# Sums of the second weights: made by adding DMAs into SBUF in the second expert phase, instead of in DRAM in the first

## The chip, the cores and the metric

One core of a Trainium2 chip. The metric is the time of one execution on the device in microseconds (us). The kernel before takes 2145.75 us, the median of 3 runs (2145.28 to 2146.46).

## The reference

`x` has 2048 rows (tokens) of 512. The kernel computes a gated mix of a Fourier transform of `x` and a mixture of eight experts in which all eight are used (K = 8 of E = 8):

```
g = sigmoid((x * gate_w).sum(-1))
a = dft_seq_re @ (x @ dft_hid_re.T) - dft_seq_im @ (x @ dft_hid_im.T)
w = softmax(x @ w_gate)                       # one weight for each of 8 experts
b = sum_e w[:, e] * (silu(x @ w1[e]) @ w2[e])  # w1: 8 x 512 x 1376, w2: 8 x 1376 x 512
out = g * a + (1 - g) * b
```

All values are float32. The matmuls run on pairs of a high and a low part: a "high" copy made by ScalarE (a Copy into float32r), a "low" remainder made by a subtraction, and three matmuls for each product (high × high, high × low, low × high). So every matmul operand costs one ScalarE instruction and one subtraction on VectorE or GpSimd.

## The kernel before

The 8 × 1376 rows of the expert weights form 86 chunks of 128 hidden units. The program runs in four stages. First the transform along the sequence (0 to 322 us of the profile), then the projections with `wd` (322 to 418 us). Then comes the **first expert phase** (418 to 1317 us): 29 rounds (`plan_round`), each of 20 fast-multiplication products (chains A to F, `SEQ`) on up to three chunks, which gives the hidden values. Each round loads its block of `w1` and makes sums and splits of it (GpSimd lines 1064 and 1079, ScalarE line 1077, loads in lines 1033, 1035 and 1070). Lines 1152 and 1178 combine the products, line 1230 copies PSUM banks that are needed again, 1168 applies the silu, and the values and their combinations are stored to DRAM in `hd` (lines 1184, 1206 and 1221).

The **second expert phase** (1317 to 2140 us) multiplies the hidden values by `w2` with a 2 × 2 Strassen–Winograd scheme. Chunks come in 43 pairs (`NPAIR`), and a matrix of weights is split into four quarters 11, 12, 21, 22, of which one block in DRAM (`w2d`) holds 128 × 512 values, enough for two pairs; there are 22 blocks (`NB2`). The seven products need these weights (`FORMS`, line 1351): product 1 takes 11, 4 takes 22, 2 takes 12, and the others take sums of quarters: s1 = 21 + 22 (product 5), s2 = s1 + 11 (product 6), s3 = 11 + 21 (product 7) and s4 = s2 + 12 (product 3). The products are computed in groups that share loads of hidden values: `GROUPS = ((1, 7), (6, 4), (3, 5), (2,))`. Within a group the loop runs over the 43 pairs; the second product of a pair follows `SKEW` = 2 pairs behind the first. One product of one pair is 12 matmuls of 128 × 512 in four PSUM banks, so a pair of a two-product group is 24 matmuls and a block of weights lasts for 48. The 12 or 24 matmuls need hidden values from DRAM (`plan_pair_h`, loads of 512 KB in line 1437, one or two for each pair; a subtraction of two of them in line 1451 for products 7, 4 and 5; splits in lines 1458 and 1462) and a block of weights (`plan_pair_w`, loads of 256 KB in line 1415, split in lines 1420 and 1425). When a group ends, its banks go to eight accumulators of 512 KB in SBUF (`accb`; the transform's part, loaded from `yd` and multiplied by the gate in line 1366): straight by VectorE, or by a ScalarE copy (line 1489) and additions on GpSimd (both line 1377). The last accumulations are stored to the output (line 1384).

**The sums before.** `plan_sums` (lines 1317 to 1345) makes s1 to s4 in DRAM (`sd`) during the first expert phase, four blocks at a time: SP copies a quarter (line 1325, 1 MB), GpSimd's queue adds another to it by an adding DMA (line 1328, `accum_op=add`), SP copies that sum as the start of the next, and so on. For each group of blocks there are four copies and four adding DMAs; two of the four copies, c2 and c4, read what an adding DMA wrote.

**What sets the order.** `Plan` (line 98) is a list scheduler that runs when the program is built: each operation has an engine, a duration, a due time, a release time `rel`, its dependencies, and buffers of a ring ("RW" for blocks of the second phase). For each engine it takes the ready operation with the earliest due time, and gives it a buffer. A DMA is taken to end `size / GBPS` after the DMAs before it, plus 2.2 us (line 277). The resulting order is written out; `pin` keeps it for ScalarE, VectorE, GpSimd (its DMAs too) and the first matmul of each triple. Loads and copies on SP aren't pinned, and can be put earlier by the layer that records the program. At run time each engine, and SP's queue, executes in order: an instruction whose wait isn't over holds everything behind it on that engine.

Of the kernel before, what the change touches and what calls it, by code (L numbers as in the profile page):

```python
# [97 lines left out]
class Plan:  # L98
# [49 lines left out]
    def run(self, t0):  # L148
# [59 lines left out]
        while left:  # L208
# [19 lines left out]
            while again:  # L228
                again = False
                for e in engines:  # L230
# [56 lines left out]
def fnet_moe_kernel(ctx: ExitStack, tc: tile.TileContext, x, xT, cT, wd, w1d, w2d, wg, out):  # L287
# [27 lines left out]
    sd = dram.tile([4, NB2, P, 2, 256], F32, name="sd")  # L315
# [11 lines left out]
    def pin(ins):  # L327
        tc.keep_in_program_order(ins)
# [986 lines left out]
    sdone = {}  # L1315

    def plan_sums(q, t):
        lo, hi = 4 * q, min(4 * q + 4, NB2)
        size = 2 * MB / 2 * (hi - lo)

        def flat(a):
            return a.rearrange("b (p r) q c -> (b p) (r q c)", r=4)

        def copy(dst, src, due, deps):
            return load(due, lambda: nc.sync.dma_start(flat(dst), flat(src)), size, deps=deps, rel=due)

        def plus(dst, src, due, deps):
            return op("POOL", 1.2, due, lambda: pin(nc.gpsimd.dma_start(flat(dst), flat(src), accum_op=add,
                                                                        max_dma_last_dim=4096)),
                      deps, rel=due, size=size)  # L1330

        S = [sd[s_, lo:hi] for s_ in range(4)]
        W11, W12, W21, W22 = (w2d[s_, lo:hi] for s_ in range(4))
# [8 lines left out]
        sdone[q] = {1: a1, 2: a2, 3: a3, 4: a4}  # L1342

    for q in range((NB2 + 3) // 4):
        plan_sums(q, T1 + 30 + 104 * q)
# [43 lines left out]
    SKEW, NEARLY = 2, 2  # L1389
    units = []  # L1390
    for gi, ms in enumerate(GROUPS):
        for p in range(NPAIR):
            units.append((gi, 0, p))
            before = (gi, p - SKEW) if p >= SKEW else (gi - 1, NPAIR + p - SKEW)
            if before[0] >= 0 and len(GROUPS[before[0]]) == 2:
                units.append((before[0], 1, before[1]))
    need_at = {u: T2 + 4 * UNIT * n for n, u in enumerate(units)}

# [4 lines left out]
    def plan_pair_w(gi, p):  # L1403
        ms, need = GROUPS[gi], need_at[gi, 0, p]
        src_, lob, hib = X("RW"), X(), X()
        lo_ = []
        for j, m in enumerate(ms):
            key = FORMS[m][1]
            dep = []
            if key[0] == "s":  # L1410
                s_ = int(key[1])
                dep, src = [sdone[p // 8][s_]], sd[s_ - 1, p // 2]
            else:
                src = w2d[("11", "12", "21", "22").index(key), p // 2]
            lo_.append(load(need - 10, lambda j=j, src=src: nc.sync.dma_start(f(src_)[:, j, :],
                                                                            src.rearrange("p q c -> p (q c)")),
                            MB, deps=dep, bufs=[src_], rel=need - 24))
# [3 lines left out]
                lo_, [src_, hib])  # L1421
        early = gi == 0 and p < 4
# [7 lines left out]
    def plan_pair_h(gi, p):  # L1430
# [10 lines left out]
        for m in ms:  # L1441
# [6 lines left out]
            early = gi == 0 and p < 3  # L1448
# [130 lines left out]
```

## Time and profile before

| | before |
|---|---|
| time, median of 3 runs | 2145.75 us |
| time of the profiled execution | 2146.88 us |
| its span (first to last instruction) | 2144.9 us |
| PE busy | 2046.7 us (95%), 8848 matmuls |
| DVE busy | 1643.6 us (77%) |
| ACT busy | 1046.0 us (49%) |
| POOL busy | 845.4 us (39%) |
| mean granted TensorE clock | 0.982 |
| DMA, mean | 233 GB/s, 500.47 MB |

PE is the TensorE's matmuls, PEld its weight loads, DVE is VectorE, ACT ScalarE, POOL GpSimd, SP the engine that issues most DMAs; PEq, SPq and POOLq are the queues of PE, SP and POOL. A row of the timeline is: start, duration, engine, line, operation, output<-inputs, shape, and in brackets the idle time before it with what ended it. Names are those of the buffers: `psp` are PSUM banks, `tc`, `tg` and `tw` temporary buffers, `wfs` split first weights, `hd`, `sd` and `w_dram` tensors in DRAM (`w_dram` stands for `w1` and `w2`), names that begin with `xf` the big SBUF buffers. The granted clock is the share of its full clock that TensorE was given. Matmuls are pipelined, so a stage is best judged by the time it takes for a count of matmuls.

### The profile page before, as it was taken

Reading aid. Unit: us, or ns where it says so; the run is one execution under the profiler, and the core shown is the slowest. Engines: PE = TensorE matmul, PEld = TensorE weight load, DVE = VectorE, ACT = ScalarE, POOL = GpSimd, SP = SyncE. Lnnn points to the kernel's source line nnn. Section 1 sums busy time; section 2 is a strip of 40 time slices with the busy share of each in tenths; the row PEclk is TensorE's granted clock in tenths of the full one; section 3 lists DMA queues with packets and bytes.
Section 4 is the critical chain, followed back from the end, with each engine's and each line's share of the span. In section 5 each row is a group of like instructions: output and inputs, shape, how many; then the busy total and the mean of one; then the engine's idle time right before and its main releaser. Section 6 shows DMA issues by size and latency. Waiting matters only on the chain.

```text
span 2144.9 us, 26751 instructions
## 1 busy us (share of the span) xinstructions
PE 2046.7 (95%) x8848; PEld 1672.3 (78%) x8848; DVE 1643.6 (77%) x1870; ACT 1046.0 (49%) x1463; POOL 845.4 (39%) x785
## 2 busy tenths in 40 slices
PE   9999999999988898989899998999999999999999
PEld 7887888777766676767778887888888888888887
DVE  8999994876856666677778877998798779877663
ACT  6545543544544444444455555544544444444442
POOL 0010100487776776777788985131140004000110
PEclk9999999999999999999999999999999999999999
DMA  9887766557676766757786559987768777877681
GB/s 359 306 311 261 243 234 220 192 171 209 190 226 184 210 184 184 224 161 222 201 247 181 195 187 331 354 278 252 229 225 274 243 237 240 292 240 241 206 323 68
DMA packets 200546, 500.47 MB, mean 233 GB/s; under 512 B 22196, under 2 KB 37044, under 8 KB 200024
## 3 DMA queue, kind: packets, MB, share of 16 engines
q1 hardware_dynamic: 194248, 475.45, 66.0%
q0 software_dynamic: 6016, 23.07, 6.5%
q8 instruction: 69, 1.13, 0.2%
q14 instruction: 69, 0.57, 0.1%
q10 hardware_dynamic: 144, 0.26, 0.1%
HBM read 391.66 MB, written 153.17 MB: 254 GB/s over the span
## 4 chain that ended last, share of the span: by engine, by line
PE 48%; DMA 2%; DVE 1%; POOL 1%; issue 0%; ACT 0%; SPq 0%; DVEq 0%; POOLq 0%; ACTq 0%
PE psp L340 16%; PE psp L344 16%; PE psp L343 16%; DMA tc<-gTd 0%; DMA hd<-tg 0%; DMA hd<-tc 0%; DMA hd<-tw 0%; DVE tc L1178 0%; POOL tg L1064 0%; POOL wfs2n L1079 0%; DVE psp L1152 0%; POOL wfs0n L1079 0%; ACT tg L1230 0%; POOL wfs1nnnn L1079 0%; DVE tc L1201 0%
## 5 line engine op out<-in xcount | busy, mean ns | idle before, releaser
L1168 ACT ACTIVATE psp<-psp 128x512 f32<-128x512 f32 x287 | 164.7, 582 | 247.5 <-DVE psp L1152 188.9
L1377 POOL TENSOR_TENSOR xfx6n<-xfx6n,tc 128x512 f32<-128x512 f32 x2 | 4.0, 1985 | 416.8 <-ACT tc L1489 416.8
L1230 ACT ACTIVATE tc<-psp 128x512 f32<-128x512 f32 x90 | 53.3, 596 | 62.4 <-PE psp L344 44.4
L1152 DVE TENSOR_TENSOR psp<-psp,tc 128x512 f32<-128x512 f32 x75 | 52.1, 696 | 29.6 <-PE psp L344 20.7
L1064 POOL TENSOR_TENSOR tc<-ras 128x256 f32<-128x256 f32 x19 | 16.5, 871 | 141.0 <-DMA ras<-w_dram 137.1
L340 PE MATMUL psp<-xfx,wfs1nnnn 128*128 128x512 f32 x104 | 44.0, 423 | 25.8 <-ACT tg L1230 12.5
L1230 ACT ACTIVATE tg<-psp 128x512 f32<-128x512 f32 x67 | 39.9, 595 | 50.5 <-PE psp L344 31.3
L1152 DVE TENSOR_TENSOR psp<-psp,tg 128x512 f32<-128x512 f32 x59 | 41.1, 697 | 28.9 <-PE psp L344 25.9
L1079 POOL TENSOR_TENSOR wfs0n<-tg,wfs0n 128x512 fp32r<-128x512 f32 x37 | 49.6, 1340 | 25.5 <-ACT wfs0n L1077 24.8
L1079 POOL TENSOR_TENSOR wfs2n<-tc,wfs2n 128x512 fp32r<-128x512 f32 x31 | 41.9, 1351 | 29.1 <-ACT wfs2n L1077 29.1
L331 POOL TENSOR_TENSOR c73011l<-cb,c73011h 128x1024 fp32r<-128x1024 f32 x1 | 2.4, 2400 | 116.9 <-ACT c73011h L337 116.9
L1152 DVE TENSOR_TENSOR psp<-psp,tw 128x512 f32<-128x512 f32 x39 | 27.2, 698 | 27.2 <-PE psp L344 15.2
L1079 POOL TENSOR_TENSOR wfs3nnn<-tc,wfs3nnn 128x512 fp32r<-128x512 f32 x32 | 43.3, 1353 | 11.8 <-ACT wfs3nnn L1077 11.8
L340 PEld LDWEIGHTS psp<-xfx,wfs1nnnn 128*128 128x128 f32 x104 | 20.9, 201 | 32.7 <-ACT tg L1230 13.6
L1178 DVE TENSOR_TENSOR tc<-psp,tg 128x512 f32<-128x512 f32 x47 | 32.2, 686 | 17.8 <-DMA hd<-tc 10.7
L1079 POOL TENSOR_TENSOR wfs1nnnn<-tc,wfs1nnnn 128x512 fp32r<-128x512 f32 x33 | 44.6, 1353 | 3.0 <-ACT wfs1nnnn L1077 3.0
L340 PE MATMUL psp<-xfx,wfs0n 128*128 128x512 f32 x100 | 39.6, 396 | 6.1 <-DVE tw L1152 3.5
L340 PE MATMUL psp<-xfx,wfs3nnn 128*128 128x512 f32 x100 | 40.8, 408 | 4.3 <-ACT tg L1230 2.9
L344 PE MATMUL psp<-xfx,wfs1nnnn 128*128 128x512 f32 x104 | 43.2, 416 | 0.0
L1064 POOL TENSOR_TENSOR tc<-tc,ras 128x256 f32<-128x256 f32 x53 | 41.6, 784 | 2.9 <-DVE psp L1152 0.8
L340 PE MATMUL psp<-xfx,wfs2n 128*128 128x512 f32 x100 | 39.5, 395 | 0.3 <-ACT psp L1168 0.2
L344 PE MATMUL psp<-xfx,wfs3nnn 128*128 128x512 f32 x100 | 39.7, 397 | 0.0
(3115 smaller groups left out, 7946.8 us busy)
## 6 DMA issues: line engine op xcount, KB each, us to landing
hd<-tc SPq DMA_DIRECT2D x172, 256.0 KB, 3.9
ca<-cT_dram SPq DMA_DIRECT2D x63, 512.0 KB, 6.1
hd<-tg SPq DMA_DIRECT2D x99, 256.0 KB, 4.1
sd<-w_dram POOLq DMA_DIRECT2D x20, 1024.0 KB, 10.6
hd<-tw SPq DMA_DIRECT2D x73, 256.0 KB, 3.6
xfx0n<-hd SPq DMA_DIRECT2D x35, 512.0 KB, 4.6
xfw1n<-hd SPq DMA_DIRECT2D x33, 512.0 KB, 4.5
xfx2n<-hd SPq DMA_DIRECT2D x33, 512.0 KB, 4.6
```

The lines of the kernel that those rows point to most:

```text
L331: pin(nc.gpsimd.tensor_tensor(*a))
L340: ins = nc.tensor.matmul(ps, lh, rh, start=start, stop=False, skip_group_check=True)
L343: nc.tensor.matmul(ps, lh, rl, start=False, stop=False, skip_group_check=True)
L344: nc.tensor.matmul(ps, ll, rh, start=False, stop=stop, skip_group_check=True)
L1064: pin(ins.tensor_tensor(low(b, j), src(x), src(y), o))
L1079: lambda: pin(nc.gpsimd.tensor_tensor(r(w)[:, 1, :], f(b), f(w)[:, 0, :], sub)), [oh] + deps, [b, w],
L1152: q = op("DVE", V, due, lambda: pin(nc.vector.tensor_tensor(f(dst), f(a[0]), f(b_[0]), o)), [a[1], b_[1]] + list(deps), [dst, a[0], b_[0]] ...
L1168: os = op("ACT", A, due, lambda: pin(nc.scalar.activation(f(dst), f(src_), AF.Silu, scale=sign)), [o0], [dst, src_])
L1178: oh = op("DVE", V, due + 1.2, lambda: pin(nc.vector.tensor_tensor(f(hb), f(dst), f(gb), OP.mult)), [os, og], [hb, dst, gb], lock=dst.ring ...
L1230: o = op("ACT", AP_, after(x), lambda: pin(nc.scalar.activation(f(b), f(bank[x[0]]), AF.Copy)), [prod[x]], [b, bank[x[0]]])
L1377: lambda: pin(ins.tensor_tensor(acc(hf, i, a, n), acc(hf, i, a, n), f(src), o)),
```

## The change

`plan_sums` and the tensor `sd` are removed. In `plan_pair_w` the block of a sum is now made in its SBUF buffer `src_`: SP loads one quarter, an adding DMA on GpSimd's queue adds another quarter from DRAM to it, and where a third term is needed (products 6 and 3), a GpSimd addition adds the block of the other product of the group, which lies in the other half of the same buffer. The groups are now (2), (1, 7), (6, 4), (5, 3), so that the phase begins with the product that needs no sum, and 5 stands ahead of 3. Loads of weights are due 18 us before the need instead of 10 and may start 30 us before instead of 24. The planner takes a DMA to land 3.0 us after its transfer instead of 2.2. In the first pairs of the phase, low parts and subtractions that were given to GpSimd go to VectorE. The accumulators are loaded from 40 us after the start of the phase instead of 60. `plan_end` gives the products their new ways to the accumulators: products 5 and 3 now come last, and product 5 is both added straight by VectorE and copied for GpSimd.

```diff
-                        finish(o, bw + 2.2)
+                        finish(o, bw + 3.0)
...
-    sd = dram.tile([4, NB2, P, 2, 256], F32, name="sd")
...
-        c1 = copy(S[0], W21, t, [])
-        c3 = copy(S[2], W11, t + 4, [])
-        a1 = plus(S[0], W22, t + 14, [c1])
-        a3 = plus(S[2], W21, t + 28, [c3])
-        c2 = copy(S[1], S[0], t + 42, [a1])
-        a2 = plus(S[1], W11, t + 56, [c2])
-        c4 = copy(S[3], S[1], t + 70, [a2])
-        a4 = plus(S[3], W12, t + 84, [c4])
...
-    FORMS = {1: ((0, None), "11"), 7: ((3, 0), "s3"), 6: ((3, None), "s2"), 4: ((3, 1), "22"), 3: ((2, None), "s4"),
-             5: ((2, 3), "s1"), 2: ((1, None), "12")}
-    GROUPS = ((1, 7), (6, 4), (3, 5), (2,))
+    FORMS = {1: ((0, None), ("11",)), 7: ((3, 0), ("11", "21")), 6: ((3, None), ("21", "11", 1)), 4: ((3, 1), ("22",)),
+             3: ((2, None), ("11", "12", 0)), 5: ((2, 3), ("21", "22")), 2: ((1, None), ("12",))}
+    GROUPS = ((2,), (1, 7), (6, 4), (5, 3))
...
-            t0 = T2 + 60 + 30 * (2 * hf + a)
+            t0 = T2 + 40 + 25 * (hf + 2 * a)
...
-    SKEW, NEARLY = 2, 2
+    SKEW, NEARLY = 2, 0
...
+        def plus(j, key, due, deps):
+            return op("POOL", 0.9, due, lambda: pin(nc.gpsimd.dma_start(f(src_)[:, j, :], block(key), accum_op=add,
+                                                                        max_dma_last_dim=4096)),
+                      deps, [src_], size=MB)
+
+        for j in sorted(range(len(ms)), key=lambda j: FORMS[ms[j]][1][-1] in (0, 1)):
+            first, *rest = FORMS[ms[j]][1]
+            o = load(need - 18, lambda j=j, first=first: nc.sync.dma_start(f(src_)[:, j, :], block(first)), MB,
+                     bufs=[src_], rel=need - 30)
+            for key in rest:
+                if key in (0, 1):
+                    o = op("POOL", G, need - 5, lambda j=j, key=key: pin(nc.gpsimd.tensor_tensor(
+                        f(src_)[:, j, :], f(src_)[:, j, :], f(src_)[:, key, :], add)), [o, made[key]], [src_], lock=True)
+                else:
+                    o = plus(j, key, need - 12, [o])
+            made[j] = o
```

Three places show how this moves instructions. In the rows, line numbers are those of each version's own file (the lines of the changed one are lower), and brackets name the semaphores waited for: `DMASW` tells of a DMA that GpSimd's queue issued, `DMAHW` of one of SP's, the others of an engine.

The first is SP's queue in the middle of the first expert phase, before: stores of `hd`, loads of the first weights and of gate rows (`gTd`), and between them the copy of one sum to the next.

```order
L1184 DMA hd<-tw_3462 128x512 [waits DMAHW1_49,DVE_49]
L1184 DMA hd<-tc_3380 128x512 [waits DMAHW2_49,DVE_49]
L1325 DMA sd<-sd 16x16384 [waits DMAHW3_49,DMASW4_49]
L1070 DMA tw_3462<-w_dram 128x256 [waits DMAHW1_49,DMAHW4_49,DVE_49,Pool_49]
L1206 DMA hd<-tg_3390 128x512 [waits DMAHW5_49,DVE_49]
L1184 DMA hd<-tg_3382 128x512 [waits DMAHW6_49,DVE_49]
```

And SP's queue at the same store of `hd`, after:

```order
L1183 DMA hd<-tw_3461 128x512 [waits DMAHW7_49,DVE_49]
L1183 DMA hd<-tc_2997 128x512 [waits DMAHW0_49,DVE_49]
L1069 DMA tg_3389<-w_dram 128x256 [waits DMAHW1_49,Pool_49]
L1205 DMA hd<-tg_3381 128x512 [waits DMAHW2_49,DVE_49]
L1183 DMA hd<-tc_3293 128x512 [waits DMAHW3_49,DVE_49]
```

The copy that waits for an adding DMA (`DMASW4`) is gone from SP's queue; the loads and stores around it stand as they did, in other buffers.

The second is GpSimd near the end of the second expert phase. Before, it holds accumulations alone:

```order
L1377 TENSOR_TENSOR xfw2n<-xfw2n,tc_2986 128x512 [waits Activation_49]
L1377 TENSOR_TENSOR xfw5n<-xfw5n,tc_2986 128x512 [waits DVE_49]
L1377 TENSOR_TENSOR xfx11n<-xfx11n,tc_2986 128x512 [waits Pool_49]
L1377 TENSOR_TENSOR xfx6n<-xfx6n,tc_2980 128x512 [waits DVE_49,Activation_49]
L1377 TENSOR_TENSOR xfx4n<-xfx4n,tc_2980 128x512 [waits Pool_49]
```

After, in group (5, 3), it holds for each block two adding DMAs (line 1380) and one addition (line 1390):

```order
L1380 DMA xfx3n<-w_dram 128x512 [waits DMAHW1_49,DVE_49]
L1380 DMA xfx3n<-w_dram 128x512 [waits DMAHW2_49]
L1390 TENSOR_TENSOR xfx3n<-xfx3n 128x512 [waits DMASW5_49,DMASW4_49]
L1380 DMA xfx4n<-w_dram 128x512 [waits DMAHW7_49,DVE_49]
L1380 DMA xfx4n<-w_dram 128x512 [waits DMAHW0_49]
L1390 TENSOR_TENSOR xfx4n<-xfx4n 128x512 [waits DMASW7_49,DMASW6_49]
```

The adding DMAs of a block wait for SP's loads, the addition waits for both adding DMAs, and the next block's adding DMAs stand behind that addition.

The third is ScalarE around the first splits of second weights. Before, at the start of the phase with group (1, 7), the split (line 1420) waits for two loads of SP:

```order
L1230 ACTIVATE tg_3390<-psp_2972 128x512 [waits DMAHW3_49,DVE_49,PE_49]
L1420 ACTIVATE xf32n<-xfw6n 128x1024 [waits DMAHW1_49,DMAHW0_49]
L1168 ACTIVATE psp_2833<-psp_2833 128x512 [waits DVE_49]
L1168 ACTIVATE psp_2968<-psp_2968 128x512 [waits DVE_49]
L1458 ACTIVATE xf16n<-xfx0n 128x1024 [waits DMAHW2_49]
```

After, the same group comes second, behind the lone product, and its split (line 1397) waits for an adding DMA; line 1433 splits hidden values:

```order
L1397 ACTIVATE xf201n<-xfx5n 128x1024 [waits DMAHW1_49,DMASW0_49]
L1433 ACTIVATE xf10n<-xfw0n 128x1024 [waits DMAHW5_49,PE_49]
L1397 ACTIVATE xf231n<-xfx3n 128x1024 [waits DMASW1_49,Activation_49]
L1433 ACTIVATE xf14n<-xfx11n 128x1024 [waits DVE_49,PE_49,Activation_49]
L1433 ACTIVATE xf211n<-xfw4n 128x1024 [waits DMAHW7_49,PE_49]
```

The wait for an adding DMA has moved from SP's queue in the first phase to GpSimd and ScalarE in the second.

More of the change, by code (lines that the diff above doesn't have):

```diff
@@ L1396, in fnet_moe_kernel @@
                 units.append((before[0], 1, before[1]))
+    units += [(len(GROUPS) - 1, 1, p) for p in range(NPAIR - SKEW, NPAIR) if len(GROUPS[-1]) == 2]
     need_at = {u: T2 + 4 * UNIT * n for n, u in enumerate(units)}
@@ L1405, in plan_pair_w, with block @@
         src_, lob, hib = X("RW"), X(), X()
[L1406 to L1417, printed above, removed]
+        made = {}
+        def block(key):
+            return w2d[("11", "12", "21", "22").index(key), p // 2].rearrange("p q c -> p (q c)")
+        def plus(j, key, due, deps):
[13 more added lines that the diff above has]
+            made[j] = o
         nf = len(ms)
@@ L1447, in plan_pair_h @@
             dst = b if keep == k else a
-            early = gi == 0 and p < 3
-            eng, ins = ("POOL", nc.gpsimd) if early else ("DVE", nc.vector)
-            summed = op(eng, 2 * G if early else V2, need - 3.4,
-                        lambda dst=dst, a=a, b=b, ins=ins: pin(ins.tensor_tensor(f(dst), f(a), f(b), sub)),
+            summed = op("DVE", V2, need - 3.4,
+                        lambda dst=dst, a=a, b=b: pin(nc.vector.tensor_tensor(f(dst), f(a), f(b), sub)),
                         [oa, ob], [a, b], lock=True)
@@ L1486, in plan_end @@
                 due = t + (2 * hf + n + 1) * UNIT + 1.5
[L1487 to L1498 removed]
+                if m == 7:
                     s_, os = snaps[1, hf, n]
@@ L1504, in plan_end @@
                         add_to(hf, 1, a, n, w_, sub, "POOL", due + 30, [ow], [w_])
-                else:
-                    (i, a), o = {4: ((1, 0), sub), 3: ((0, 1), add), 2: ((0, 0), add)}[m]
-                    q = add_to(hf, i, a, n, bk, o, "DVE", due, [pe], [bk])
-                    if m == 2:
-                        store(hf, i, a, n, due + 1, q)
+                    continue
+                direct = {2: (0, 0, add), 4: (1, 0, sub), 5: (0, 1, sub), 3: (0, 1, add)}
+                spread = {1: ((0, 0, add), (0, 1, add)), 6: ((0, 1, sub), (1, 0, add), (1, 1, add)), 5: ((1, 1, add),)}
+                if m in spread:
+                    s_ = Buf("T")
+                    os = op("ACT", AP_, due, lambda s_=s_, bk=bk: pin(nc.scalar.activation(f(s_), f(bk), AF.Copy)), [pe],
+                            [s_, bk])
+                    snaps[m, hf, n] = (s_, os)
+                if m in direct:
+                    i, a, o = direct[m]
+                    q = add_to(hf, i, a, n, bk, o, "DVE", due, [pe], [bk])
+                    if m == 3:
+                        store(hf, i, a, n, due, q)
+                for i, a, o in spread.get(m, ()):
+                    q = add_to(hf, i, a, n, s_, o, "POOL", due + (1 if m == 5 else 30), [os], [s_])
+                    if (m, i, a) in ((1, 0, 0), (6, 1, 0), (5, 1, 1)):
+                        store(hf, i, a, n, due + 40, q)
     for gi, j, p in units:
@@ L1517, in fnet_moe_kernel @@
     for gi, ms in enumerate(GROUPS):
-        for j in sorted(range(len(ms)), key=lambda j: ms[j] not in (4, 3)):
+        for j in sorted(range(len(ms)), key=lambda j: ms[j] != 4):
             plan_end(gi, j)
```

33 lines of the change are left out of this document (2 added, 31 removed).

## The prediction

> **What bounds the kernel now.** The first view to read is the table of stretches: time, busy us and count of instructions of PE, PEld, DVE, ACT and POOL, granted PE clock, DMA share, GB/s. The first expert phase runs from 418 to 1317 us, the second from there to 2140.
>
> ```profile
> 0.00:322.40 322.40, 317.95 (x1397) 259.65 (x1398) 298.41 (x401) 166.40 (x210) 15.17 (x16) 1.00 0.82 285
> ...
> 418.00:1106.00 688.00, 609.89 (x2545) 490.45 (x2543) 470.21 (x657) 332.77 (x599) 510.18 (x526) 0.95 0.69 199
> 1106.00:1300.00 194.00, 193.43 (x849) 158.88 (x850) 156.33 (x220) 109.02 (x197) 170.14 (x171) 1.00 0.63 200
> 1300.00:1345.00 45.00, 39.39 (x169) 31.00 (x168) 35.69 (x38) 25.08 (x30) 23.90 (x10) 1.00 1.02 352
> 1345.00:2140.40 795.40, 795.40 (x3509) 658.38 (x3508) 622.45 (x509) 373.88 (x382) 107.90 (x52) 1.00 0.74 246
> ```
>
> TensorE is the bound where nothing disturbs it: 795.40/3509 = 0.2267 us a matmul in the second phase, 194.00/849 = 0.2285 late in the first. From 418 to 1106 a matmul takes 688.00/2545 = 0.270. The same rounds run in both parts of the first phase, so something in the earlier part costs 688.00 − 2545 × 0.2285 = 106.5 us. Who makes PE wait there, and who makes the load queue of SP wait (us in total, times, longest), from 440 to 1106:
>
> ```profile
> SPq L1325 <- DMA sd<-w_dram: 73.9, 10, 9.4
> PE psp L340 <- ACT tg L1230: 32.4, 8, 6.7
> PE psp L340 <- ACT tc L1230: 19.2, 6, 7.4
> PE psp L340 <- ACT tw L1230: 16.1, 5, 8.3
> ```
>
> Ten times SP, which issues in order, stands still for an adding DMA before it may copy one sum to the next (L1325). One of the ten in the timeline, SP, ACT and PE (start, duration, in brackets the idle time and who ended it):
>
> ```profile
> 839.51 0.32 SPq L1184 DMA_DIRECT2D hd<-tc  x1
> 849.10 0.47 SPq L1325 DMA_DIRECT2D sd<-sd  x1
> 849.74 0.46 SPq L1070 DMA_DIRECT2D tw<-w_dram  x1
> ...
> 855.98 0.63 ACT L1077 ACTIVATE wfs3nnn<-tw 128x512 fp32r<-128x512 f32 x1 [9.06 <-DMA tw<-w_dram]
> ...
> 857.98 0.60 ACT L1230 ACTIVATE tw<-psp 128x512 f32<-128x512 f32 x1 [0.89 <-POOL wfs3nnn L1079]
> ...
> 858.62 0.80 PE L340 MATMUL psp<-xf221n,wfs2n 128*128 128x512 f32 x1 [8.27 <-ACT tw L1230]
> ```
>
> SP issues nothing from 839.5 to 849.1; the first-weight load behind the copy (849.74) arrives for ACT at 856; ACT, in order too, then empties a PSUM bank late, and PE has been idle for 8.27 us. The clock follows:
>
> ```profile
> 850.00:858.60 8.60, 0.35 (x2) 0.00 (x0) 0.00 (x0) 1.74 (x4) 2.29 (x3) 0.66 0.90 281
> 858.60:863.00 4.40, 4.38 (x10) 3.47 (x11) 1.98 (x3) 2.19 (x4) 4.32 (x6) 0.50 0.63 200
> ```
>
> After it, ten matmuls take 4.40 us, 0.44 each at a granted clock of 0.50. From 1106 to 1290 PE waits once:
>
> ```profile
> PE psp L340 <- ACT tg L1230: 1.5, 1, 1.5
> ```
>
> **The change part by part.** *First phase.* All 24 adding DMAs (L1328) and 24 copies (L1325) go; SP keeps nothing in this phase that waits for an adding DMA, as the SP order shows. Next in line behind the removed stall are the ordinary waits for DVE and ACT, which the part after 1106 already has without loss. So I take the rate of that part: **−106.5 us**. Bounds: at the second phase's 0.2267 it is 688.00 − 577.0 = −111; if four or five stalls of 2 to 3 us have other causes (new order, gate rows, stores), −95. The 12 copies that SP now issues during the transform save nothing: PE is busy there for 317.95 of 322.40 us.
>
> *What the second phase gets.* 88 adding DMAs of 256 KB: 22 blocks in (1,7), 22 in (6,4), 44 in (5,3). 44 additions on GpSimd (22 each in (6,4) and (5,3)). The bytes loaded are the same, each sum being replaced by a block of weights. An adding DMA of 256 KB into SBUF is not in the trace. Its neighbours (KB, us from issue to landing), then the GpSimd instruction itself (ns):
>
> ```profile
> sd<-w_dram POOLq DMA_DIRECT2D x20, 1024.0 KB, 10.6
> sd<-w_dram POOLq DMA_DIRECT2D x4, 512.0 KB, 6.2
> xfw1n<-sd SPq DMA_DIRECT2D x12, 256.0 KB, 4.0
> L1328 POOL DMA_DIRECT2D sd<-w_dram x24: 802/882/1021, 463.1 to 1163.2; - x24
> ```
>
> It lies between 4.0 (a plain load, and also the line through 10.6 and 6.2 carried on to 256 KB) and 6.2; the far end is 10.6, if size were not what counts. I take 5, nearer the plain load of the same size. The Trainium skill ("DMA: Bandwidth & Descriptors", section "Anatomy of one DMA — SWDGE (gpsimd) path") fits 2.0 us plus the bytes at 436 GB/s, an estimate of 2.6 us here; for 1 MB that gives 4.4, where the row has 10.6, so the trace disagrees. By it the start of (1,7) below would cost 2.6 instead of 5, and the sum would be 2 us lower.
>
> Is there time? A block serves two pairs, that is 2 × 24 = 48 matmuls × 0.2267 = 10.9 us in a group of two products. Its load and its use now:
>
> ```profile
> 1922.60 0.91 SPq L1415 DMA_DIRECT2D xfw1n<-sd  x2
> ...
> 1937.20 1.04 ACT L1420 ACTIVATE xf17n<-xfw1n 128x1024 fp32r<-128x1024 f32 x1
> ```
>
> 14.6 us from issue to the split. The new chain is load 4.0, add 5, GpSimd addition 2.3 (below): 11.3, so 3.3 us are left. The waiting instructions are on GpSimd, with only sums and accumulations behind them, and then on ACT (L1397), with every split of the phase behind it, and then PE. In the middle of a group I therefore cost it at nothing; without that cover each late us of a block is a us of PE. The group starts are different.
>
> *Start of the phase.* Now 45.00 us for 169 matmuls, 45.00 − 169 × 0.2267 = 6.7 lost, at a DMA share of 1.02 and with two loads of `hd`, a sum and a subtraction for each pair. The lone product needs one load, no sum and no subtraction: half the loss, **−3.4** (0 to −6.7).
>
> *Start of (1,7).* Eight accumulators of 512 KB and four gate rows are loaded inside the lone group, from the same ring of buffers, and the first two blocks must then also be added to. I charge one add in full: **+5** (0 to 10.6).
>
> *Starts of (6,4) and (5,3).* GpSimd runs in order, and now carries weights as well as accumulations, whose duration at the end of a group is (ns, min/median/max)
>
> ```profile
> L1377 POOL TENSOR_TENSOR xfw5n<-xfw5n,tc x3: 2267/2275/2280, 1567.4 to 1805.6; 128x512 f32<-128x512 f32 x3
> 1565.00:1780.00 215.00, 215.00 (x950) 178.09 (x949) 174.44 (x145) 101.48 (x101) 15.88 (x8) 1.00 0.76 248
> ```
>
> After (1,7) come 16 accumulations, 36.4 us; with three weight additions (6.8) and three issues (2.6) that is 45.8 us of GpSimd in three block times (32.7): 13.1 late, less the 3.3 spare: 9.8. Some accumulations yield to weights, so half: **+5** (0 to 10). After (6,4) come 12: 27.3 + 6.8 + 5.3 = 39.4, 6.7 late, 3.4 net. There the DMA engines are nearly full as well (rival 1), so in all **+4** (0 to 8). DVE, 174.44 of 215.00 us busy, loses about 1 us to each addition: 44 in some 468 us takes 81% to 90%, still hidden. Two stalls long enough for the half clock: **+2** (0 to 5).
>
> *End.* The last product again ends in DVE additions and stores:
>
> ```profile
> 2140.50 1.01 SPq L1384 DMA_DIRECT2D out_dram<-xfx3n  x2
> ```
>
> There the four accumulations of product 5 on GpSimd (9.1 us) start some 8 us before PE ends, so they end about when DVE does: 0 (to +2).
>
> **Sum.** −106.5 − 3.4 + 5 + 5 + 4 + 2 = −93.9. The profiled execution took 2146.9, 1.1 over the median of 2145.75: 2146.9 − 93.9 − 1.1 = 2051.9, say **2052**.
>
> **Rivals.** *1: the DMA engines bound (5,3).* Queue, packets, MB and share of 16 engines: the second phase alone, then the adds over the whole span.
>
> ```profile
> q1 hardware_dynamic: 65079, 195.00, 73.8%
> ...
> q0 software_dynamic: 6016, 23.07, 6.5%
> ```
>
> A loaded MB costs 0.738 × 795 / 195 = 3.0 us of all engines, an added one 0.065 × 2144.9 / 23.07 = 6.0. A block time of (5,3) has 2.62 MB of loads (7.9) and 0.52 MB of adds (3.1): 11.0 of 10.9 us. (1,7) and (6,4) have 7.9 + 1.6 = 9.5. For it: no spare at all. Against it: the 3.0 holds waiting too; the row from 1300 to 1345 moves 352 GB/s. If adds and loads hinder each other by 10 to 20%, 22 blocks lose 1.1 to 2.2 each, 24 to 48 us: 2076 to 2100. The Trainium skill (the same page, section "Queues, rings and completion order") has each engine take turns between the queues that have work, packet by packet, so an add does slow a load beside it; no run here shows it yet.
>
> *2: the first phase keeps half of its loss,* because the late bank copies have a second cause, stores of `hd` or gate rows on a queue that is now ordered with a longer assumed latency. For it: ten SP stalls, but 19 waits of PE for ACT. Against: a stall is followed by more than one wait, and there is only one after 1106. 2052 + 53 = 2105.
>
> *3, slower: the chain on GpSimd becomes the bound.* The order below has add, add, addition, then the next block's adds. If an add into SBUF takes 10.6 us, 0.9 + 10.6 + 2.3 = 13.8 us a block; beyond 10.9 it decides, 2.9 × 44 = 128 us. 2052 + 128 = 2180. Against: size has counted so far (6.2 for half).
>
> *4: group starts cost nothing,* and the first phase runs at 0.2267: 2146 − 111 − 3 = 2032.
>
> **How the numbers follow.** Forecast 0.58, rival 1 0.18, rival 2 0.09, rival 3 0.04, rival 4 0.11. Low end: rival 4 with the whole loss at the start of the phase gone, 2146 − 111 − 6.7 = 2028. High end: the forecast with all its upper bounds, 2052 + 11.5 (first phase) + 3.4 + 5.6 + 5 + 4 + 3 + 2 (the terms of the second, in their order) = 2086, and it takes in the lower part of rival 1. Left out: rivals 2, 3 and half of 1, 0.22. Faster by over 0.2% (about what a measurement of this kernel can tell from no change) 0.95, within it 0.01, slower 0.04.
>
> **What would show it.** Right: from 418 on 0.227 to 0.230 us a matmul and a clock of 1.00 throughout the first phase, no SP wait for an adding DMA, the first phase about 105 us shorter; in the second, short gaps at three group starts, ACT L1397 waiting there for a DMA of `w_dram` or for GpSimd. Wrong: gaps spread evenly through (5,3) at a DMA share near 1 (rival 1); L1230 waits before 1106 (rival 2); adds landing after 8 us or more (rival 3).

## The result and the profile after

| | before | after |
|---|---|---|
| median | 2146.11 us, 4 runs (2145.28 to 2147.45) | 2044.94 us, 4 runs (2044.01 to 2046.57) |
| after / before, 95% interval | | 0.9529 (0.9512 to 0.9545) |
| span of the profiled execution | 2144.9 | 2044.7 |
| projections | 95.9 | 97.2 |
| first expert phase, 3456 matmuls | 898.6 (260.0 ns each) | 788.2 (228.1 ns) |
| second expert phase, 3612 matmuls | 823.9 (228.1 ns) | 833.3 (230.7 ns) |
| behind the last matmul | 4.5 | 4.3 |

Times are in us. The stages run from the start of the first matmul of their kind to the end of the last. The first phase is 110.4 us shorter, the second 9.4 longer, the projections 1.3 longer. The changed kernel takes 101 us less; forecast were 94 less, 2052, with a range of 2028 to 2086.

The head of the page after:

```profile
PE 2019.8 (99%) x8848; PEld 1660.9 (81%) x8848; DVE 1664.5 (81%) x1883; ACT 1044.8 (51%) x1463; POOL 960.7 (47%) x880
...
q1 hardware_dynamic: 193480, 452.38, 64.4%
q0 software_dynamic: 12672, 23.07, 6.9%
```

PE is now busy for 99% of the span. The adding DMAs (queue q0) still move 23.07 MB, in more and smaller packets; SP's queue q1 moves 23 MB less than before, the copies.

The table of stretches after, the first expert phase and then the four groups of the second:

```profile
419.00:1207.30 788.30, 785.85 (x3458) 647.22 (x3458) 634.54 (x893) 451.74 (x812) 676.59 (x673) 1.00 0.56 185
1207.30:1324.00 116.70, 115.75 (x509) 95.21 (x509) 76.51 (x73) 56.61 (x64) 29.93 (x19) 1.00 0.92 329
1324.00:1558.00 234.00, 231.16 (x1018) 190.72 (x1017) 190.76 (x163) 114.75 (x115) 24.43 (x26) 1.00 0.87 274
1558.00:1792.00 234.00, 230.43 (x1005) 190.19 (x1004) 203.06 (x152) 106.95 (x105) 93.05 (x62) 0.99 0.88 273
1792.00:2040.50 248.50, 246.50 (x1084) 202.79 (x1082) 200.55 (x157) 108.87 (x112) 103.55 (x74) 1.00 0.83 255
```

The first phase has no slow part any more, and its granted clock is 1.00. In the second the DMA share is between 0.83 and 0.92 and PE loses 1 to 4 us in each stretch. PE's longest waits over the whole of after, apart from those of the projections:

```profile
PE psp L339 <- DVE tw L1465: 3.6, 1, 3.6
PE psp L342 <- DVE xf30nn L1437: 2.3, 2, 1.3
...
PE psp L343 <- DVE xf12nn L1402: 1.5, 1, 1.5
```

All three name VectorE, not ScalarE waiting for a block of weights. How the 88 new adding DMAs of 256 KB land:

```profile
DMA to landing us min/median/max: 4.0/6.7/9.8
```

The one large new stall, at 1571 us in group (6, 4) (timeline of after, rows of PE left out up to the last):

```profile
1563.62 0.88 POOL L1380 DMA_DIRECT2D xfx0n<-w_dram  x1 [4.36 <-DMA xfx0n<-w_dram]
1564.23 1.59 POOL L1344 TENSOR_TENSOR xfw6n<-xfw6n,tc 128x512 f32<-128x512 f32 x1
1564.40 8.70 DVE L1437 TENSOR_TENSOR xf31n<-xf200nn,xfx 128x1024 fp32r<-128x1024 f32 x1
1565.59 1.48 POOL L1344 TENSOR_TENSOR xfx8n<-xfx8n,tc 128x512 f32<-128x512 f32 x1
...
1570.61 1.40 POOL L1344 TENSOR_TENSOR xfw6n<-xfw6n,tw 128x512 f32<-128x512 f32 x1
...
1574.17 0.68 DVE L1465 TENSOR_TENSOR tw<-psp,tc 128x512 f32<-128x512 f32 x1
...
1574.90 0.79 PE L339 MATMUL psp<-xf10n,xf15n 128*128 128x512 f32 x1 [3.57 <-DVE tw L1465]
```

GpSimd issues an adding DMA and then does six additions without a break; a subtraction of VectorE that otherwise takes 1.22 us starts during the issue and takes 8.70, ending 1.1 us after the sixth addition. The bank behind it is emptied late, PE stops for 3.57 us, and the granted clock is half for 6.8 us (from 1573.9 on).

### The profile page after: what moved, and what is told of

Same layout as the page of the kernel before. It is cut to its first block, busy times and chain, and to the rows that moved or that the text cites. A ratio compares the mean times of both kernels' runs of the same rounds, so it can differ in the third digit from the quotient of the medians.

```text
span 2044.7 us, 26840 instructions
## 1 busy us (share of the span) xinstructions
PE 2019.8 (99%) x8848; PEld 1660.9 (81%) x8848; DVE 1664.5 (81%) x1883; ACT 1044.8 (51%) x1463; POOL 960.7 (47%) x880
## 3 DMA queue, kind: packets, MB, share of 16 engines
q0 software_dynamic: 12672, 23.07, 6.9%
## 4 chain that ended last, share of the span: by engine, by line
PE 92%; DVE 4%; DMA 2%; issue 1%; POOL 0%; ACT 0%; SPq 0%; DVEq 0%; ACTq 0%; POOLq 0%
PE psp L342 26%; PE psp L339 26%; PE psp L343 26%; PE u L342 5%; PE u L339 5%; PE u L343 5%; DVE xfw L1437 0%; DMA xfw0n<-hd 0%; DMA hd<-tg 0%; DMA ca<-cT_dram 0%; DMA tg<-gTd 0%; DMA xfx0n<-w_dram 0%; DMA xfw5n<-hd 0%; DMA tw<-gTd 0%; DVE xf30nn L1437 0%
## 5 line engine op out<-in xcount | busy, mean ns | idle before, releaser
L1151 DVE TENSOR_TENSOR psp<-psp,tc 128x512 f32<-128x512 f32 x84 | 58.6, 698 | 37.7 <-PE psp L343 30.5
L1390 POOL TENSOR_TENSOR xfx3n<-xfx3n 128x512 f32<-128x512 f32 x12 | 28.4, 2363 | 51.7 <-DMA xfx3n<-w_dram 51.7
L1151 DVE TENSOR_TENSOR psp<-psp,tg 128x512 f32<-128x512 f32 x47 | 32.8, 699 | 22.5 <-PE psp L343 19.2
L1229 ACT ACTIVATE tw<-psp 128x512 f32<-128x512 f32 x55 | 32.7, 597 | 26.3 <-PE psp L343 23.6
L339 PE MATMUL psp<-xfx,wfs3nnn 128*128 128x512 f32 x118 | 46.0, 389 | 0.0
L343 PE MATMUL psp<-xfx,wfs3nnn 128*128 128x512 f32 x118 | 45.9, 389 | 0.0
L339 PE MATMUL psp<-xfx,wfs0n 128*128 128x512 f32 x116 | 45.1, 389 | 0.0
L343 PE MATMUL psp<-xfx,wfs0n 128*128 128x512 f32 x116 | 45.1, 389 | 0.0
L343 PE MATMUL psp<-xfx,wfs2n 128*128 128x512 f32 x114 | 44.4, 389 | 0.0
L339 PE MATMUL psp<-xfx,wfs2n 128*128 128x512 f32 x114 | 44.4, 389 | 0.0
L1390 POOL TENSOR_TENSOR xfx4n<-xfx4n 128x512 f32<-128x512 f32 x11 | 23.4, 2123 | 43.6 <-DMA xfx4n<-w_dram 43.6
L1229 ACT ACTIVATE tg<-psp 128x512 f32<-128x512 f32 x52 | 31.1, 597 | 21.8 <-PE psp L343 17.7
L1078 POOL TENSOR_TENSOR wfs0n<-tc,wfs0n 128x512 fp32r<-128x512 f32 x27 | 35.9, 1328 | 10.9 <-ACT wfs0n L1076 10.7
```

The costliest lines, as they stand in the source:

```text
L339: ins = nc.tensor.matmul(ps, lh, rh, start=start, stop=False, skip_group_check=True)
L343: nc.tensor.matmul(ps, ll, rh, start=False, stop=stop, skip_group_check=True)
L1078: lambda: pin(nc.gpsimd.tensor_tensor(r(w)[:, 1, :], f(b), f(w)[:, 0, :], sub)), [oh] + deps, [b, w],
L1151: q = op("DVE", V, due, lambda: pin(nc.vector.tensor_tensor(f(dst), f(a[0]), f(b_[0]), o)), [a[1], b_[1]] + list(deps), [dst, a[0], b_[0]] ...
L1229: o = op("ACT", AP_, after(x), lambda: pin(nc.scalar.activation(f(b), f(bank[x[0]]), AF.Copy)), [prod[x]], [b, bank[x[0]]])
L1390: o = op("POOL", G, need - 5, lambda j=j, key=key: pin(nc.gpsimd.tensor_tensor(f(src_)[:, j, :], f(src_)[:, j, :], f(src_)[:, key, :], add ...
```

## The experiments

The theory on record was that SP's queue, standing still for copies that wait for adding DMAs (line 1325), made the whole loss of the first phase. The first three experiments start from the kernel before.

**E1: the planner's latency alone.**

```diff
-                        finish(o, bw + 2.2)
+                        finish(o, bw + 3.0)
```

> The kernel before with one edit: the planner takes a DMA to land 3.0 us after its transfer instead of 2.2. Theory (SP's queue stands behind copies that wait for adding DMAs): the copies stay where they were, so nothing is gained: 2130 to 2155 us, ten or so SP waits of L1325 for an adding DMA, 60 to 80 us in all. Rival (the new order of the first phase, planned with the longer latency, brought the gain): 2045 to 2090 us.

Measured: 2152.38 us, 1.0014 of before (1.0000 to 1.0028). In the kernel with the sums in the first phase the latency is worth nothing.

**E2: the copies kept at their planned place.** The 12 copies c2 and c4 are held where the planner put them in SP's queue, behind their adds' landing by the plan. No bytes change.

```diff
-            return load(due, lambda: nc.sync.dma_start(flat(dst), flat(src)), size, deps=deps, rel=due)
+            def go():
+                ins = nc.sync.dma_start(flat(dst), flat(src))
+                if deps:
+                    pin(ins)
+
+            return load(due, go, size, deps=deps, rel=due)
```

> The kernel before, but the 12 copies of one sum to the next are kept at their planned place in SP's queue, some 20 us behind the adding DMA that they read, instead of being put forward. All bytes of the sums, copies and adds, stay in the first phase. Theory (the queue's standstill): the first phase falls to 0.228 to 0.232 us a matmul, the whole to 2030 to 2050 us. Rival (the bytes of the sums hinder the phase's own transfers): the standstill goes but most of the loss stays, 2090 us or more. The planner's latency is the old one here, so a fall also speaks against the new order as a cause.

Measured: 2109.77 us, 0.9812 (0.9795 to 0.9830): 40 us less than the 2149.92 of before beside it. SP's waits for adds, 73.9 us in ten before, are down to one of 9.4, but PE's three longest waits from 440 to 1106 still come to 46.6 us, from 67.7:

```profile
SPq L1326 <- DMA sd<-w_dram: 9.4, 1, 9.4
```

```profile
PE psp L340 <- ACT tc L1230: 22.7, 9, 7.1
PE psp L340 <- ACT tg L1230: 16.8, 8, 3.9
PE psp L340 <- ACT tw L1230: 7.1, 4, 3.0
```

The standstill was real and cost 40 us, but more than half of the loss outlived it. The theory doesn't hold as the whole cause.

**E3: copies that need no sum.** c2 and c4 copy a quarter instead of a sum; they wait for no add and SP issues them all during the transform.

```diff
-        c2 = copy(S[1], S[0], t + 42, [a1])
+        c2 = copy(S[1], W22, t + 42, [a1])
...
-        c4 = copy(S[3], S[1], t + 70, [a2])
+        c4 = copy(S[3], W22, t + 70, [a2])
```

> The kernel before, but the 12 copies take a quarter of the weights instead of the sum before, so that they wait for no adding DMA (the sums s2 and s4 are then others than the reference's). Their bytes now move earlier, in the transform; the 24 adding DMAs stay in the first phase. Theory: 2030 to 2050 us, no SP wait of L1325. Rival that the adding DMAs themselves, 23 MB at twice the cost of a load, slow the phase: 2080 us or more.

Measured: 2092.42 us, one run; 17 less than E2. What leaves the phase against E2 is 12 copies with their bytes, and the last stall of SP. All adds remain, and so do waits of PE. One of them in the timeline, DVE, POOL, ACT and PE:

```profile
867.37 0.69 DVE L1152 TENSOR_TENSOR tc<-tg,psp 128x512 f32<-128x512 f32 x1 [7.30 <-DMA hd<-tc]
...
868.14 0.74 POOL L1064 TENSOR_TENSOR tg<-ras 128x256 f32<-128x256 f32 x1 [4.96 <-DVE tc L1152]
...
868.70 0.58 ACT L1168 ACTIVATE psp<-psp 128x512 f32<-128x512 f32 x1 [7.09 <-DVE psp L1152]
...
873.72 0.79 PE L340 MATMUL psp<-xfx,wfs1nnnn 128*128 128x512 f32 x1 [3.94 <-ACT tg L1230]
```

VectorE wants a temporary buffer again whose store to `hd` hasn't landed; ScalarE and GpSimd stand behind it, and PE last. So I measured from the traces how long a DMA of SP takes from issue to landing between 440 and 1200 us, when an add is under way half a microsecond after the issue starts and when none is (medians, us, of those whose landing the trace gives):

| | beside an add | no add |
|---|---|---|
| stores of `hd`, before | 7.05 | 3.41 |
| loads of first weights, before | 7.03 | 3.22 |
| stores of `hd`, E3 | 6.82 | 2.70 |
| stores of `hd`, after (no add in the phase) | | 2.42 |

The Trainium skill ("DMA: Bandwidth & Descriptors", section "Queues, rings and completion order") has each DMA engine take turns between its queues packet by packet. By that a store beside a 1 MB add lands late; with 7 against 3 us the runs here agree.

**E9: the same with the later latency.** E3 with `bw + 3.0`.

> As the run with copies of quarters (no copy waits for an adding DMA), with the planner's latency at 3.0 instead of 2.2 us (s2 and s4 are others than the reference's). The 24 adding DMAs run in the first phase. Theory A (the adds' bytes): 2080 to 2100 us, as with 2.2. Theory B' (the order was planned too tight for the real landings): 2070 us or less.

Measured: 2093.28 us, 0.9739 (0.9723 to 0.9755), as E3.

**E7: sums planned but not made.** The planner keeps its times and slots for copies and adds, but none is issued; the second phase loads quarters in their place.

```diff
-            return load(due, lambda: nc.sync.dma_start(flat(dst), flat(src)), size, deps=deps, rel=due)
+            return load(due, lambda: None, size, deps=deps, rel=due)
...
-            return op("POOL", 1.2, due, lambda: pin(nc.gpsimd.dma_start(flat(dst), flat(src), accum_op=add,
-                                                                        max_dma_last_dim=4096)),
-                      deps, rel=due, size=size)
+            return op("POOL", 1.2, due, lambda: None, deps, rel=due, size=size)
```

> The kernel before with the sums still in the plan, with their sizes and times, but no copy and no adding DMA issued; the second phase loads quarters in place of sums (its output is not the reference's). With the standstill gone, 40 to 57 us were gained, and some 55 us of the first phase were left. Theory A (the bytes of the adds and copies hinder the phase's own transfers): without them the first phase runs at 0.228 us a matmul, 2030 to 2045 us. Theory B (the order, planned around the sums, makes the waits): 2075 us or more, with PE gaps at the same places, 594, 629, 694 and 718 us.

Measured: 2043.50 us, 0.9511 (0.9497 to 0.9525). The copies and adds as issued are the whole of the loss, not the slots that the plan holds for them.

**E8: neither planned nor made.** `plan_sums` isn't called.

> The kernel before with no sums, neither planned nor issued, with the old latency of 2.2 us in the planner and the old order of the groups; the second phase loads quarters in place of sums (its output is not the reference's). Both theories: first phase at 0.228 to 0.231 us a matmul, 2030 to 2050 us. If it is 2055 or more, the planner's longer latency has a share in the gain that shows only when the sums are gone.

Measured: 2043.44 us, 0.9511 (0.9497 to 0.9525), as E7.

From before to E7 the first phase gets its loss back in three parts: SP's standstill 40 us (E2), the copies c2 and c4 in the phase, with the last stall, 17 (E3), and the 24 adding DMAs 50 (E9 to E7): 107 in all. Some seven tenths of it are waits of TensorE and the rest its clock: in the profiled first phases it is idle for 80.2 us in before and 7.6 in E7, and its matmuls take 818.5 us at a granted clock of 0.96, and 789.2 at 1.00.

**E10: adds cut small.** E3 with 88 adds of 256 KB instead of 24, nearly all of 1 MB, to learn whether the adds cost by their length. The copies are cut in the same way, and 54 of the 88 are issued in the first phase (419 to 781 us), where E3 has none: the run changes two things.

```diff
-        lo, hi = 4 * q, min(4 * q + 4, NB2)
+        lo, hi = q, q + 1
...
-    for q in range((NB2 + 3) // 4):
-        plan_sums(q, T1 + 30 + 104 * q)
+    for q in range(NB2):
+        plan_sums(q, T1 + 30 + 26 * q)
```

> As the run with copies of quarters, but each adding DMA of the first phase has 256 KB instead of 1 MB, and there are four times as many (88, as in the changed kernel's second phase): the same bytes in the same phase, in bursts a quarter as long (s2 and s4 are others than the reference's). Theory (a store of hidden values that meets a long add lands 4 us late, 7 instead of 3, and the first phase has no buffers to spare for that; short adds delay it by little): most of the 49 us goes, 2045 to 2070 us, stores beside an add at 5 us or less. Rival (the engine time of the adds counts, however it is cut): 2080 to 2105 us.

Measured: 2120.75 us, 0.9865 (0.9851 to 0.9880): 28 us slower than with 24 adds, and outside both expectations. A store of `hd` beside an add does land earlier, in 4.64 us, but more of them meet one (133 of 230, against 66 of 220 in E9). Among PE's waits those for GpSimd in the splits of first weights have grown, to 18.8 us in three rows, from 4.2 in E9 (420 to 1250 us):

```profile
PE psp L344 <- POOL wfs0n L1079: 8.5, 6, 2.9
PE psp L344 <- POOL wfs3nnn L1079: 5.7, 3, 4.4
...
PE psp L344 <- POOL wfs1nnnn L1079: 4.6, 3, 4.1
```

How much of the 28 us belongs to the number of adds and how much to the 54 copies, this run doesn't tell.

**E12: adds without bytes.** E3, its 24 adds as they are, and 66 adding DMAs of 64 × 16 bytes, about as many as E10 has more than E3, spread over the first phase. No copy moves: all 24 stay in the transform.

```diff
+        for k in range(3 * (hi - lo)):
+            n = 12 * q + k
+            op("POOL", 1.2, t + 8.7 * k + 6,
+               lambda n=n: pin(nc.gpsimd.dma_start(tiny[n], w2d[0, 0, 0:64, 0, 0:4], accum_op=add)),
+               [], rel=t + 8.7 * k + 6, size=0.001)
```

> The kernel whose second and fourth copy start from quarters (2092.42 us, latency no matter), with 24 adding DMAs of 1 MB as there and, spread over the first phase, 66 more adding DMAs of 64 x 16 bytes into a scratch tensor that nothing reads: the instructions on GpSimd of the kernel with 88 small adds, without its many copies on SP and without more bytes. Theory A, GpSimd's time: an issue holds GpSimd for about 0.8 us, 66 of them for 53 us, on an engine that is busy for 690 of 831 us there and makes the low parts of the first weights; the loss of the 88 small adds against the 24 large ones (28 us) comes back whole or nearly: 2110 to 2125, with PE waiting some 20 us for GpSimd in the splits of first weights. Theory B, the many adds and copies with bytes delay more stores and loads: small transfers delay nothing, 2090 to 2100, and PE waits under 8 us for GpSimd.

Measured: 2174.29 us, 1.0119 (1.0096 to 1.0142): 82 us slower than E3, 1.24 us for each tiny add, where an issue shows 0.78 us on GpSimd (median). Theory B falls. Theory A has the direction and its sign (PE's waits for GpSimd in the splits of first weights, 19.1 us against 6.4 in E3), but not the size. The first phase as a row of the table of stretches, E3 and then E12:

```profile
417.80:1260.82 843.02, 801.48 (x3458) 648.96 (x3457) 630.72 (x886) 454.06 (x813) 695.72 (x704) 0.99 0.68 201
417.19:1340.12 922.93, 831.80 (x3458) 664.35 (x3457) 653.18 (x886) 455.92 (x813) 739.59 (x771) 0.96 0.65 185
```

TensorE is idle for 91.1 us instead of 41.5: 50 more, or 0.75 for each tiny add, about what an issue takes. The other 30 us are matmuls that take longer, at a granted clock of 0.96 instead of 0.99. So what the time of the issues leaves over is mainly the half clock after the waits. Part of the waits comes through VectorE; how much isn't shown (timeline of E12, POOL and DVE):

```profile
1089.60 1.24 DVE L1178 TENSOR_TENSOR tw<-tw,tc 128x512 f32<-128x512 f32 x1
...
1090.23 0.77 POOL L1346 DMA_DIRECT2D tiny<-w_dram  x1
...
1090.78 1.53 POOL L1079 TENSOR_TENSOR wfs3nnn<-tg,wfs3nnn 128x512 fp32r<-128x512 f32 x1
...
1090.87 5.31 DVE L1201 TENSOR_TENSOR tw<-tg,tw 128x512 f32<-128x512 f32 x1
...
1092.04 0.97 POOL L1064 TENSOR_TENSOR tg<-ras,tc 128x256 f32<-128x256 f32 x1
```

It is the stall of 1571 us again: an operation of VectorE with both inputs in SBUF that starts during or right after an issue of GpSimd's queue takes 5.31 us instead of 1.24, while GpSimd goes on without a break. From 440 to 1150 us E12 has 12 such instances over 2.5 us, 11 of them within 1.3 us of the start of an issue; E3 and before have 8 each, all at an issue; after, without an issue there, has none. On the mean, an operation of VectorE that overlaps an issue takes 1025 ns in E12, and the others 731; a long one is also more likely to overlap an issue.

E10 and E12 have nearly the same number of issues (88 and 90), and E10, without long adds, is 54 us faster, although it has copies in the phase. So adds cost without any length (E12 against E3), and long ones most likely cost more than short ones; E10 and E12 issue them at other places, too. The parts don't simply add: 24 issues at 1.24 us would be 30 of the 50 us from E9 to E7, and 54 for length would be over twice the rest. How the 50 divide stays open.

The other four runs start from the kernel after.

**E4: the lone product last.** GROUPS is (1, 7), (6, 4), (5, 3), (2), and the stores of the output follow the new order.

```diff
-    GROUPS = ((2,), (1, 7), (6, 4), (5, 3))
+    GROUPS = ((1, 7), (6, 4), (5, 3), (2,))
```

> The changed kernel with the old place of the lone product: groups (1,7), (6,4), (5,3), (2); the outputs of product 2 are then the last to be stored. Theory (the lone product eases the start, worth 3 to 4 us there, and gives the first adds time): 2 to 12 us slower than the changed kernel, 2047 to 2057, lost in the first 40 us of the second phase. Rival (the order of the groups is worth nothing, all the gain is the removal of the sums from the first phase): within 2 us of 2045.

Measured: 2054.80 us, 0.9564 (0.9544 to 0.9584), 10 slower than after. Beginning with product 2 is worth that. The seam between the phases costs three gaps here, 2.7, 1.5 and 5.0 us, where after has one of 0.9; the first phase takes 797.0 us against 788.2, and the second by itself is as long (833.9 against 833.3).

**E5: no adding DMA at all.**

```diff
-                    o = plus(j, key, need - 12, [o])
+                    pass
```

> The changed kernel without its 88 adding DMAs in the second phase (the sums then lack those quarters); the loads and the 44 additions on GpSimd stay. Theory (adds are hidden in the middle of groups and cost some us at the starts of groups): 2 to 6 us faster, 2039 to 2043, DMA share of the last group down from 0.83 to about 0.72. Rival (the adds hinder the second phase all along, the 9 us by which it is longer than before): 8 us or more faster, 2037 or less.

Measured: 2040.33 us, 0.9498 (0.9483 to 0.9513). The 88 adds cost 4.6 us where they now are, against 50 for 24 in the first phase. No addition or subtraction of VectorE takes over 2.5 us in this run's second phase; after has seven, up to 9.3. The run of GpSimd's additions at the start of group (6, 4) is there all the same (timeline of E5, DVE, POOL and PE):

```profile
1566.62 2.27 POOL L1344 TENSOR_TENSOR xfw6n<-xfw6n,tw 128x512 f32<-128x512 f32 x1
1567.66 2.31 DVE L1437 TENSOR_TENSOR xfx<-xfx11n,xfw 128x1024 fp32r<-128x1024 f32 x1
1568.86 2.26 POOL L1344 TENSOR_TENSOR xfx8n<-xfx8n,tg 128x512 f32<-128x512 f32 x1
1569.90 2.31 DVE L1437 TENSOR_TENSOR xf221nn<-xfw4n,xf32n 128x1024 fp32r<-128x1024 f32 x1
...
1572.86 0.50 PE L339 MATMUL psp<-xf211n,xf201n 128*128 128x512 f32 x1 [1.93 <-DVE tw L1465]
```

Without an issue the two engines take turns: VectorE needs 2.31 us for what takes 1.22 alone, and GpSimd 2.27 for what takes 1.4 in after, while VectorE is held up. VectorE still loses 1.1 us to each addition, and PE still stops for 1.93 us at the same place, with no adding DMA at all.

**E6: accumulations with breaks between them.** The accumulations of GpSimd that follow groups (1, 7) and (6, 4) are released 5.5 us apart; nothing else changes.

```diff
+    last = [0.0]
+
+    def spaced(due):
+        last[0] = max(last[0] + 5.5, due + 3)
+        return last[0]
...
-                        add_to(hf, 1, a, n, w_, sub, "POOL", due + 30, [ow], [w_])
+                        add_to(hf, 1, a, n, w_, sub, "POOL", due + 30, [ow], [w_], rel=spaced(due))
...
-                    q = add_to(hf, i, a, n, s_, o, "POOL", due + (1 if m == 5 else 30), [os], [s_])
+                    q = add_to(hf, i, a, n, s_, o, "POOL", due + (1 if m == 5 else 30), [os], [s_],
+                               rel=None if m == 5 else spaced(due))
```

> The changed kernel, with the accumulations on GpSimd after (1,7) and (6,4) released one every 5.5 us of the plan instead of all at once. The stall of 3.6 us at 1571 us, with 6.8 us of half clock behind it, came while one VectorE subtraction took 8.7 us beside six GpSimd additions in a row. Theory (a run of GpSimd additions holds VectorE up, which then frees a PSUM bank late): that stall goes, and the kernel is 4 to 8 us faster, 2037 to 2041. Rival (the bank is late because of the order of work at the group's end, whatever GpSimd does): the stall stays, within 2 us of 2045.

Measured: 2037.76 us (2036.66 to 2038.43), 0.9486 (0.9471 to 0.9501). It is faster than both kernels, by 7.2 us than after. Groups (6, 4) and (5, 3) in its table of stretches:

```profile
1558.00:1792.00 234.00, 234.00 (x1034) 193.77 (x1033) 199.16 (x156) 111.25 (x112) 95.10 (x63) 1.00 0.89 279
1792.00:2032.10 240.10, 240.10 (x1060) 198.48 (x1058) 200.76 (x154) 104.82 (x106) 92.20 (x73) 1.00 0.85 259
```

PE has no gap in either, at a DMA share of 0.89 and 0.85 and with all 88 adds: the stall at 1571 us came from the run of additions, not from the adds' landing. Behind the same issue (1563.23 us) there are two additions instead of six, and VectorE's operation takes 3.42 us instead of 8.70. It is still held up nine times for over 2.5 us, 6.6 at most, but no wait of PE comes of it. The second phase takes 824.3 us. With all its adds the kernel is 2.6 us faster than E5, which has none but keeps the run of additions.

**E11: the same with the old latency.** E6 with `bw + 2.2`.

> The run with spaced accumulations, with the planner's latency back at 2.2 us. The runs so far show no gain from 3.0 in the first phase, and some 1.5 us more of gaps in the projections (393 to 412 us) with it. Theory: 2034 to 2038, the gaps in the projections back to those of before; the second phase has the lead to stand the shorter latency. Rival (the second phase needs 3.0 for its adds): 2042 or more, with new gaps at the starts of its groups.

Measured: 2044.09 us, 0.9515 (0.9494 to 0.9537). The later latency is worth 6 us here, as the rival had it, but not where it looked: the second phase takes 824.3 us with either, the first 794.2 against 788.1. PE's waits from 419 to 1215 us in E11, and in E6:

```profile
PE psp L339 <- ACT tg L1229: 3.4, 2, 2.6
PE psp L339 <- ACT psp L1167: 2.7, 2, 1.5
```

```profile
PE psp L339 <- DVE tw L1177: 1.3, 1, 1.3
PE psp L339 <- ACT psp L1167: 0.9, 1, 0.9
```

The first 2545 matmuls of the phase take 585.4 us in E11, and 584.9 and 586.1 in E7 and E8, which have the old latency too; they take 581.2 in E6 and 581.4 in after. The latency isn't all that E7 and E8 lose, whose first phases take 797 and 798 us. The last 62 matmuls of the phase take 5.0 us longer in E7 than in after, 2.3 in E8, and 7.7 in E4, which has the later latency: in all three group (1, 7) follows.

## Why the prediction was right, and where its reasons were not

**First phase, −106.5: measured −110.4.** The size was right, and within its bounds (−95 to −111). The step that failed is the one ahead of it: "Ten times SP, which issues in order, stands still for an adding DMA before it may copy one sum to the next", taken for the whole loss. It carries 40 of the 107 us (E2). The rest is 17 for the copies c2 and c4 in the phase, with the last stall, and 50 for the adding DMAs. With adds under way, stores of `hd` and loads of first weights land in 7 us instead of 3, GpSimd's time is taken, and VectorE is held up; how the 50 divide among these isn't shown. Rival 2 named a second cause, stores of `hd`, and it exists; but it came from the sums too, so the change removed it along with the first, and the 53 us of that rival did not remain. The sum held because it was made by comparing two stretches, before and after 1106 us: almost all the copies and adds end there, not SP's stall alone. The argument "a stall is followed by more than one wait" for the 19 waits of PE was wrong: 46.6 of 67.7 us of them were still there in E2, with one stall left.

The row from 418 to 1106 was priced at 0.2285 us a matmul, and its matmuls now take just that, 581.4 us in place of 688.0:

```profile
419.05:1000.44 581.39, 578.94 (x2546) 476.26 (x2545) 468.63 (x657) 332.66 (x600) 507.33 (x505) 1.00 0.55 181
```

That it is met so closely is in part luck: some 4 us of it come from the later latency (E11 against E6), which the sum had at nothing and of which rival 2 expected a loss. The other 3.8 of the 110.4 us came in the 911 matmuls behind it, 206.8 us instead of 210.6.

**The second phase, +12.6 in all: measured +9.4.** *Start of the phase, −3.4:* the 169 matmuls around it took 45.0 us and take 40.0 now, so −5.0, inside the bounds; with group (1, 7) ahead they take 53.6 (E4). *Start of (1, 7), +5:* two gaps, 1.5 and 1.3, at 1326 and 1333 us; they wait for VectorE's low parts of second weights and hidden values, which it works off without a break, not for an add. *Start of (6, 4), +5:* the place was right, and the accumulations of GpSimd stood there, with a stop of 3.6 us; but what they held up was VectorE, not the weight additions. The sum let VectorE lose about 1 us to each addition, which E5's rows bear out where no adding DMA is issued. Behind an issue it lost 7.5 us at once. E6 shows it by taking it away. *Start of (5, 3), +4:* gaps of 0.8 and 1.0. *Half clock, +2:* at most 3.4, half of 6.8 us, all at (6, 4). *End, 0:* 4.3 us behind the last matmul, from 4.5. The 1.3 us of the projections were not in the sum.

**An add of 256 KB, 5 us:** 6.7 at the median and 9.8 at most, above the range of 4.0 to 6.2 but under the far end of 10.6; 11 of the 88 took 8 us or more. The load, add and addition stayed within the lead, since no wait of PE names them. The estimate of 2.6 us by the fit of the Trainium skill ("DMA: Bandwidth & Descriptors", section "Anatomy of one DMA — SWDGE (gpsimd) path") falls shorter still, and the trace disagrees with it here too.

**The rivals.** 1 (DMA engines bound): no gap in (5, 3) in E6 at a share of 0.85; it was overrated. 3 (GpSimd's chain): its sign, adds that land after 8 us, is there in 11 of 88, but no wait of PE goes back to the landing of an add, and it did not come about. 4 (starts at no cost, 2032): nearer to E6's 2037.76 than to the change.

**The signs.** The rate, the clock, the end of SP's waits, and the shorter first phase came as named. The sign for the group starts came in part: ScalarE's line 1397 does wait for GpSimd's weight additions (2.5 us at 1790, 5.8 at most), but PE's waits there are for VectorE.

## What to carry to other kernels

Two stretches of one program, with and without a piece of work, price everything that the piece does; the longest wait in the list tells where it is first seen, not that it is all of it, so undo the wait alone before giving it the whole sum. A DMA issued by GpSimd has a price beside its bytes: 66 that moved next to nothing cost 82 us in a phase in which GpSimd was busy for 696 of 843 us without them (E3), and 88 of 256 KB cost 4.6 in one in which it was busy for 177 of 833 (E5). So it belongs in a phase in which GpSimd's work has breaks. Where GpSimd does a row of additions behind such an issue, spread them. And look at the clock before a loss is put down to an engine: in E12 30 of 80 us were matmuls at the lower clock that followed the waits.

## What the runs showed of the hardware that was not expected

*An issue on GpSimd's queue can shut VectorE out until GpSimd next pauses.* In after, the subtraction at 1564.40 ends at 1573.1, and GpSimd's run of additions behind the issue at 1572.0; one of 9.3 us follows at 1816.5, 0.5 us after an issue, and GpSimd did seven additions in a row behind that one. E4 has two more, of 10.48 and 11.59 us, behind which GpSimd did seven and eight additions; the second makes PE stop for 4.06 us. Each of the four ends 1.1 us after GpSimd's last addition, as if it began there: alone it takes 1.2. In E12 one starts at 483.89, during an issue, and ends at 487.9, with GpSimd's run ending at 487.4. Such instances go where the issues go: none over 2.5 us in the second phase of E5, where the two engines take turns, 2.3 us for each operation. The Trainium skill ("SBUF — State Buffer", section "Who interferes with whom") has a VectorE operation with two inputs in SBUF contend with a GpSimd instruction that reads SBUF, over ports that are locked for one of them. The runs agree on who contends, and E5's turns fit a lock for one instruction; behind an issue VectorE was out over six. The same section infers that such an operation doesn't meet the writing of descriptors. The stalls at E12's issues, which move next to nothing, speak against it. Why an issue opens such a stretch was not tried.

*Small adds in place of long ones, with their copies cut too, made it slower,* 2120.75 against 2092.42 us (E10), although a store beside one landed sooner: 4.64 us in place of 6.74. The 54 copies that moved into the phase have a share in it that wasn't measured apart.
